# A retention block and a gated MLP on one core: decays 2 and 3 and four weight loads on GpSimd, and a new order of loads

## The chip, the cores and the metric

One NeuronCore of a Trainium2 chip. The metric is the device time of one execution in microseconds (us); times given for the kernel are the median of several runs. A profile is one execution, recorded instruction by instruction. Its engines are PE (TensorE: matmuls; PEld is its weight load), DVE (VectorE), ACT (ScalarE), POOL (GpSimd) and SP (SyncE, which here only issues transfers).

## The reference

Attention by a recurrence over 768 positions, for 4 batches and 8 heads of width 64, and behind it a two-layer MLP with a quick GELU. All values are float32; the program is given the two weight matrices as float64 and narrows them itself on the chip.

```python
def _attn_ref(q, k, v):
    B, H, S, D = q.shape                                    # 4, 8, 768, 64
    gamma = 1.0 - 2.0 ** (-5.0 - np.arange(H, dtype=np.float32))
    scale = 1.0 / np.sqrt(D)
    state = np.zeros((B, H, D, D), dtype=np.float32)
    for t in range(S):
        state = gamma[None, :, None, None] * state + np.einsum('bhd,bhe->bhde', k[:, :, t], v[:, :, t])
        y[:, :, t] = scale * np.einsum('bhd,bhde->bhe', q[:, :, t], state)
...
def _moe_ref(x, w_in, w_out):                               # x: 3072 x 512, from y
    h = x @ w_in                                            # 512 x 2048
    g = h * (1.0 / (1.0 + np.exp(-1.702 * h)))
    return (g @ w_out).astype(np.float32)                   # 2048 x 512
```

## The kernel before

**Attention** goes in 24 steps `j`, each 64 positions of two batches: steps 0 to 11 are the first two batches, 12 to 23 the others. Four steps make a block of 512 tokens for the MLP. A step is made of these pieces, whose names stand in the written order below:

- `q`, `k`, `v` load its operands (`load`, L139). For steps 0 to 5 the keys come as four transfers of 64 KB, the queries as one of 256 KB, the values as two of 128 KB. From step 6 on (`NEW`) queries and keys come already cut for a 32 by 32 transpose on VectorE, in eight transfers each of 32 KB made of 128-byte pieces (L176); there `q6` loads queries and keys together, and `v6` loads the keys once more in natural order (`kn`, four transfers) and the values (four), both at L161.
- `turn_q`, `turn_k` (steps 0 to 5) transpose on TensorE (L283); `turned_q`, `turned2_q`, `turned_k` copy the results out (L300), the second quarter pair of the queries on VectorE. `turn6`, `turn7` are VectorE's transposes (L294).
- `decay` weights the keys by their distance from the step's end: on ScalarE it is eight activations, one for each head (L323), on GpSimd one multiplication (L318; L325 from step 6).
- `score` (L339) multiplies keys and queries; `masked` (L380) takes the scores out under the causal decay mask; `own` (L367) multiplies them with the values; `gain` (L347) makes the step's addition to the state; `past` (L358) reads the state.
- `state` (L387) scales what `past` made, `x` (L409) adds it to `own` and writes the MLP's input; `aged` (L421, L418 or L423) decays the state, `updated` (L432) adds the gain.

Scores, gains, `past` and `own` use two fixed PSUM tiles (`PAS`, `PYS`), so a piece that writes one waits until the step before has been read out.

**The weights** come as 16 chunks of w_in and w_out, two transfers of 512 KB each (`w0a`, `w0b`, ... `w15b`, L201), into three raw buffers that are used in turn. Chunks 0 to 7 are w_in, 8 to 15 w_out. A chunk is narrowed by `abs` (L237) and `low` (L241) on ScalarE and `clip` (L245), `lift` (L248), `sign` (L253) and `rest` (L258) on VectorE. The raw buffer is free again once `sign` and `low` have read it. Chunk `i` of w_in holds two of the 16 strips of the hidden layer: chunks 0 to 7 are strips pairs 2, 7, 3, 6, 0, 4, 5 and 1.

**The MLP's first layer** of the first two blocks runs between these pieces: `up0.h.p` (L476) is a half block times strip pair `p`, `gate0.h.p` its GELU on ScalarE (L457); `seven` and `zero` (L559, L599) do the same with seven products in place of eight, from sums of weights (`seven_4`, `seven_6`, `seven_52`, L508 to L518) and of inputs (`zero_x` L546, `seven_x` L500). `seven_keep` (L538) stores such sums to DRAM. The second layer and all later blocks (L698, L821, L954) follow behind.

**What sets the order.** The pieces of the first 150 us stand in a list written by hand, one name after the other; `name@engine` puts a piece on another engine. Each engine executes its own instructions in the order of that list and waits by semaphores for what others make; so an instruction that waits holds up all that stands behind it on the same engine. Loads stand on SP, if the list doesn't say otherwise; they wait there for their buffer, and, with eight transfer semaphores used in turn, for the eighth transfer before them. The keys of step 0 are issued by ScalarE. A transfer that GpSimd issues has a queue of its own (q0), those of SP share q1. GpSimd in the first 110 us has the causal mask, the decays of steps 0 and 1, the small `whole` loads (L1035), `anew` (L1045 to L1053: a small load and copies that bring masks, decays and state into the layout of step 6 on) and from there decays and ages of the state.

Of the kernel before, what the change touches and what calls it, by code (L numbers as in the profile page):

```python
# [28 lines left out]
def kernel(  # L29
# [29 lines left out]
    pe, act, dve, pool, sp = nc.tensor, nc.scalar, nc.vector, nc.gpsimd, nc.sync  # L59
# [43 lines left out]
    row = G[0:1, 4, 0:2].rearrange("p a (h t) -> p (a h) t", t=D)  # L103
# [6 lines left out]
    mask = const.tile([P, 2, HP, D], F32, name="mask")  # L110
# [32 lines left out]
    def load(j, what="qkv", engine=None):  # L143

        b, c = j // NC * 2, j % NC
        rows = slice(c * D, (c + 1) * D)
        keep = send if j < 2 * CB else lambda i: i

        def plain(name, src, tag, bufs, engine=sp):
            t = two.tile([P, H, D], F32, name=name + "_in", tag=tag, bufs=bufs)
            QKV[name, j] = t
            for i in range(2):
                if j < NEW:
                    to, at = t[i * D:(i + 1) * D], src[b + i, :, rows, :].rearrange("h p d -> p h d")
                    for n in range(1 if name == "v" else 2):
                        keep(engine.dma_start(*((to, at) if name == "v" else (to[:, n:H:2], at[:, n * HP:(n + 1) * HP]))))
                else:
                    for r in range(2):  # L160
                        keep(engine.dma_start(t[r * D:(r + 1) * D, i * HP:(i + 1) * HP],  # L161
                                              src[b + i, r * HP:(r + 1) * HP, rows, :].rearrange("h p d -> p h d")))

        if j < NEW:
            if "q" in what:
                QKV["q", j] = t = two.tile([P, H * D], F32, name="q_in", tag="q_sq", bufs=2)
                keep((engine or sp).dma_start(t, q[b:b + 2, :, rows, :].rearrange("i h (k p) d -> (i h) k (p d)", p=8)))
            if "k" in what:
                plain("kn", k, "k_sq" if j in (0, 1, 4, 5) else "o", 2, engine or pool)
        elif "q" in what:  # L170
            for name, src in (("q", q), ("k", k)):
                t = two.tile([P, H, D // C4, C4], F32, name=name + "_sq")
                for r0 in range(0, P, C4):
                    for n in range(D // C4):
                        t0 = c * D + n * C4
                        tc.keep_in_program_order(sp.dma_start(  # L176
                            t[r0:r0 + C4, :, n], src[b + r0 // D, :, t0:t0 + C4, r0 % D:r0 % D + C4]
                            .rearrange("h p d -> p h d")))
                QKV[name, j] = t
        if "v" in what:  # L180
            if j >= NEW and c < NC - 1:
                plain("kn", k, "kn", 1)
            plain("v", v, "v", 2, engine or sp)
# [102 lines left out]
    def turn(j):  # L286

        if j < NEW:
            turn_new(j, 1)
            turn_new(j, 0)  # L290
        else:
            QT[j], KT[j] = home(j, "qT"), home(j, "kT")
            for t, name in ((QT[j], "q"), (KT[j], "k")):
                tc.keep_in_program_order(dve.transpose(  # L294
                    t.rearrange("p h t -> p (h t)"), QKV.pop((name, j)).rearrange("p h n d -> p (h n d)")))
        if 2 * CB <= j < NCH - 2:
            load(j + 2, "qk")
# [136 lines left out]
    def step(j, f=None):  # L434
        attend(j, f)
        if j is not None:
            masked(j)
            if j > 2 * CB:
                decay(j)
        if f is not None:  # L440
            c = f % NC
            if c == 0:
                updated(f)
            else:
                by_state(f)
            output(f)
            if 0 < c < NC - 1:
                aged(f)
                updated(f)
        if j is not None and 2 * CB < j < NCH - 1:  # L450
            load(j + 1, "v")
# [587 lines left out]
    def late_loads():  # L1039
        load(2 * CB, "qkv")  # L1040
        load(2 * CB + 1, "qk")
# [61 lines left out]

    begin()
    for name in """
        row@sp k0@act table q0 v0 z5 rows turn_q0 turn_k0 q1 w0b k1@sp w0a mask causal turned_q0
        turned2_q0@dve turned_k0 decay0@pool score0 v1 turn_k1 turn_q1 masked0 gain0 turned_k1 turned_q1 turned2_q1@dve own0 abs0b low0b updated0
        decay1@pool score1 clip0b lift0b sign0b rowd whole q2 k2@sp masked1 abs0a low0a rest0b x0 past1 gain1
        clip0a lift0a sign0a own1 rest0a aged1 turn_k2 turn_q2 w2b w2a state1 updated1 x1 turned_k2 turned_q2 turned2_q2@dve
        v2 q3 k3@sp up0.0.2 score2 abs2 decay2 aged2@dve q4 clip2 lift2 sign2 low2 decay3 w3b w3a  # L1110
        masked2 turn_k3 turn_q3 k4@sp gain2 past2 own2 v3 q5 rest2 k5@sp gate0.0.2 turned_k3 turned_q3 turned2_q3@dve updated2
        state2 score3 decay4 low3 turn_q4 turn_k4 up0.0.3 x2 masked3 gain3 past3 own3 abs3 clip3 lift3 sign3
        turned_q4 turned2_q4@dve rest3 turned_k4 score4 turn_k5 turn_q5 up0.0.6 w1a w5b w1b aged3 updated3 state3 w5a v4
        x3 up0.1.3 turned_q5 turned2_q5@dve gate0.0.3 abs1 low1 abs5 clip1 aged4 lift1 sign1 masked4 own4 gain4 w6a
        rest1 clip5 lift5 gate0.0.6 sign5 up0.0.7 past4 w6b decay5 low5 rest5 updated4 v5 gain5 w4a abs6
        gate0.1.3 turned_k5 clip6 state4 x4 lift6 score5 masked5 w4b abs4 up0.1.7 low6 aged5 gate0.0.7 w7a w7b
        low7 low4 q6 sign6 v6 own5 rest6 past5 seven_4.2 state5 gate0.1.7 seven_6.2 updated5 zero2.0 clip4 up0.1.6
        lift4 sign4 x5 seven_52.2 rest4 turn6 anew decay6 abs7 aged6 up0.1.2 w8a gate0.1.2 clip7 zero_x zero2.1
        score6 past6 q7 w8b v7 zero2.2 masked6 lift7 sign7 gain6 rest7 own6 w11b zero2.3 zero2.4 turn7
        w9a updated6 aged7 gate0.1.6 zero2.5 decay7 zero2.6 state6 w11a seven_4.0 x6 zero0.0 score7 masked7 abs8 clip8  # L1120
        past7 zero0.1 state7 seven_6.0 seven_52.0 lift8 sign8 gain7 own7 x7 seven_x zero0.2 zero0.3 zero0.4 zero0.5 low8
        seven_keep.2 w9b abs9 low11 clip9 rest8 lift9 zero0.6 w10a seven2.0 w10b seven2.1 abs11 clip11 lift11 sign11
        seven_4.1 rest11 seven2.2 abs10 seven2.3 seven2.4 seven_w.1 clip10 lift10 sign9 seven0.0 seven2.5 low10 low9 rest9 sign10
        updated7 rest10 seven_4.3 seven2.6 seven0.1 seven0.2 seven0.3 seven0.4 seven1.0 seven_keep.0 w14b w14a w12b w12a abs12 seven_w.3
        clip12 seven0.5 seven0.6 seven_v.1 lift12 sign12 abs14 clip14 low12 rest12 lift14 sign14 seven1.1 seven1.2 w13a seven1.3
        w13b abs13 low14 seven_v.3 clip13 lift13 seven1.4 sign13 seven3.0 seven1.5 rest14 seven1.6 seven3.1 seven3.2 seven3.3 seven3.4
        w15a seven_keep.3 seven_keep.1 w15b abs15 clip15 lift15 low13 low15 sign15 seven3.5 rest13 seven3.6 rest15 late_loads
    """.split():
        name, *e = name.split("@")
        works[name](*[{"sp": sp, "pool": pool, "act": act, "dve": dve}[x] for x in e])  # L1130
# [109 lines left out]
```

## Time and profile before

| | |
|---|---|
| median of 3 runs | 650.57 us (649.11 to 650.8) |
| the profiled execution | 651.44 us, of it 649.7 us span |
| HBM read and written | 79.18 MB and 14.94 MB |
| SP's queue q1 | 138,048 packets, 42.83 MB, 30.2% of 16 engines' span |
| GpSimd's queue q0 | 8,672 packets, 40.00 MB, 19.3% |
| weight transfers of 512 KB on SP, issue to landing | 4.8 us in the median |
| key transfers of 64 KB on SP | 4.8 us |
| SP waiting for the buffers of chunks 4 and 7 | 5.2 us before 49.19, 3.6 us before 53.71 |

A row of the profile's groups or timeline names the line, the engine, the operation, the written and read tiles, the shape and how often it runs; in square brackets stands the idle time of the engine just before, and what seemed to end it. A wait for several engines is put down to the one that finished last in the profile, which need not be the one that is waited for. The granted clock is the share of TensorE's full clock.

In the chain that ended last TensorE holds 83%, transfers 9%, SP's issuing 5%, waits for nothing visible 1%, VectorE 1%. Of the first 110 us much of that chain lies on SP's queue; from 103 us on it is TensorE almost alone.

### The profile page before, as it was taken

How to read it: one execution, taken by the hardware profiler on the slowest of the kernel's cores; microseconds unless marked ns; L12 is line 12 of the kernel's file. 1: busy time of each engine (PE TensorE's matmuls, PEld its weight loads, DVE VectorE, ACT ScalarE, POOL GpSimd, SP SyncE). 2: the span in 40 equal slices, each digit the busy share in tenths (PEclk: the TensorE clock that was granted, in tenths of full speed). 3: DMA queues.
4: the chain of work that ended last, by engine and by line, in shares of the span. 5: the costliest groups of instructions: out<-in, count | busy, mean ns of one | idle time of the engine just before them, and what ended most of it. 6: DMA issues, size and time to landing. Idle time of an engine off the chain costs nothing.

```text
span 649.7 us, 15510 instructions
## 1 busy us (share of the span) xinstructions
PE 633.4 (97%) x6543; PEld 578.4 (89%) x6543; DVE 435.6 (67%) x643; ACT 184.4 (28%) x329; POOL 152.0 (23%) x184
## 2 busy tenths in 40 slices
PE   7899999999999998999999999999999999999997
PEld 4788888888889997889999889999888999888997
DVE  2879887979989962438874337985246976145854
ACT  3778237661001102332101333100333110233210
POOL 4000211300612435000645000635300425200000
PEclk9989999999999999999999999999999999999999
DMA  9995587783368875720667730667741354221143
GB/s 198 228 258 161 112 252 214 198 209 57 93 200 264 206 175 171 200 67 4 172 179 213 215 85 1 160 161 189 211 95 49 89 174 143 110 91 49 59 153 98
DMA packets 150710, 96.86 MB, mean 149 GB/s; under 512 B 130512, under 2 KB 135888, under 8 KB 149616
## 3 DMA queue, kind: packets, MB, share of 16 engines
q1 hardware_dynamic: 138048, 42.83, 30.2%
q0 software_dynamic: 8672, 40.00, 19.3%
q10 hardware_dynamic: 3920, 13.04, 5.4%
q8 instruction: 51, 0.84, 0.6%
q14 instruction: 19, 0.16, 0.1%
HBM read 79.18 MB, written 14.94 MB: 145 GB/s over the span
## 4 chain that ended last, share of the span: by engine, by line
PE 83%; DMA 9%; SPq 5%; issue 1%; DVE 1%; ACT 1%; ACTq 0%
PE pq L821 33%; PE px L698 17%; PE pz L698 9%; PE pd L954 7%; PE ph L599 6%; PE py L698 4%; DMA W<-in_moe_w_out_dram 2%; SPq L161 2%; PE pa L339 2%; DMA q_in<-in_q_dram 2%; DMA kn_in<-in_k_dram 2%; DMA LATE<-W1D 1%; SPq L176 1%; PE py L367 1%; PE pa L347 1%; DMA v_in<-in_v_dram 1%
## 5 line engine op out<-in xcount | busy, mean ns | idle before, releaser
L821 PE MATMUL pq<-W,G 128*128 128x128 f32 x840 | 100.3, 276 | 0.0
L821 PEld LDWEIGHTS pq<-W,G 128*128 128x128 f32 x840 | 97.0, 192 | 0.8
L796 POOL DMA_DIRECT2D LATE<-W2D x34 | 18.7, 551 | 260.5 <-PE pq L821 139.8
L821 PE MATMUL pq<-LATE 128*128 128x128 f32 x560 | 74.8, 277 | 0.0
L821 PEld LDWEIGHTS pq<-LATE 128*128 128x128 f32 x560 | 68.2, 192 | 0.6
L698 PE MATMUL px<-X,LATE 128*128 128x256 f32 x256 | 60.6, 380 | 2.2 <-DMA LATE<-W1D 2.2
L698 PE MATMUL px<-X,W1A 128*128 128x256 f32 x256 | 60.5, 379 | 0.0
L698 PEld LDWEIGHTS px<-X,LATE 128*128 128x128 f32 x256 | 48.6, 190 | 9.1 <-issue 2.6
L698 PEld LDWEIGHTS px<-X,W1A 128*128 128x128 f32 x256 | 48.4, 190 | 6.3
L743 DVE TENSOR_TENSOR G<-pz,vv 128x512 f32<-128x512 f32 x16 | 11.1, 692 | 51.5 <-ACT vv L713 51.5
L843 ACT ACTIVATE o<-pq 128x512 f32<-128x512 f32 (+1 forms) x18 | 9.8, 544 | 119.9 <-PE pq L821 94.3
L457 ACT ACTIVATE G<-G 128x512 f32<-128x512 f32 x49 | 30.9, 630 | 43.1 <-DVE G L753 19.7
L821 PE MATMUL pq<-LATE,G 128*128 128x128 f32 x280 | 37.0, 275 | 0.0
L821 PE MATMUL pq<-W,LATE 128*128 128x128 f32 x280 | 37.0, 275 | 0.0
L954 PE MATMUL pd<-W,LATE 128*128 128x256 f32 x160 | 35.1, 380 | 0.0
L821 PEld LDWEIGHTS pq<-W,LATE 128*128 128x128 f32 x280 | 34.1, 192 | 0.0
L821 PEld LDWEIGHTS pq<-LATE,G 128*128 128x128 f32 x280 | 34.1, 192 | 0.0
L954 PEld LDWEIGHTS pd<-W,LATE 128*128 128x128 f32 x160 | 30.4, 190 | 4.1
L683 DVE TENSOR_TENSOR G<-G 128x512 f32<-128x512 f32 (+2 forms) x28 | 15.9, 567 | 23.5 <-ACT G L457 23.5
L810 DVE TENSOR_TENSOR LATE<-G 128x512 f32<-128x512 f32 x35 | 27.6, 789 | 5.0 <-PE pq L821 2.2
L476 PE MATMUL ph<-X,W1A 128*128 128x256 f32 x128 | 30.6, 397 | 0.2 <-DVE X L409 0.2
L698 PE MATMUL pz<-X,W1A 128*128 128x256 f32 x128 | 30.3, 380 | 0.0
(214 smaller groups left out, 1163.5 us busy)
## 6 DMA issues: line engine op xcount, KB each, us to landing
LATE<-W2D POOLq DMA_DIRECT2D x34, 768.0 KB, 5.2
W<-in_moe_w_out_dram SPq DMA_DIRECT2D x12, 512.0 KB, 6.0
LATE<-W1D ACTq DMA_DIRECT2D x4, 1536.0 KB, 9.7
LATE<-W1D POOLq DMA_DIRECT2D x4, 1536.0 KB, 8.9
kn_in<-in_k_dram SPq DMA_DIRECT2D x84, 64.0 KB, 4.8
W<-in_moe_w_in_dram SPq DMA_DIRECT2D x10, 512.0 KB, 4.8
out_dram<-o POOLq DMA_DIRECT2D x20, 256.0 KB, 4.6
q_sq<-in_q_dram SPq DMA_DIRECT2D x144, 32.0 KB, 3.0
```

Of the source, the lines that this page charges most:

```text
L161: keep(engine.dma_start(t[r * D:(r + 1) * D, i * HP:(i + 1) * HP], src[b + i, r * HP:(r + 1) * HP, rows, :].rearrange("h p d -> p h d")))
L339: pe.matmul(PAS[HALF[w], u, 0, s, :], kt[HALF[u], w, s, :], qt[HALF[u], w, s, :], start=True, stop=True)
L457: pin(act.activation(g, h[:, i], AF.Gelu_apprx_sigmoid))
L476: pe.matmul(h[:, ab], w, X[:, 2 * th + c // 2, c % 2, :], start=(ab == 0 and c == 0), stop=(c == 3), skip_group_check=True)
L599: pe.matmul(acc[:, u, :], w, x, start=(start and u == 0 and c == 0), stop=(stop and c == 1), skip_group_check=True)
L683: hold(dve.tensor_sub(q[0][1], q[0][0], q[0][1]))
L698: pe.matmul(acc[:, u, :], w1(2 * d + u, sw)[:, c, :], X[:, sx, c, :], start=(start and u == 0 and c == 0), stop=(stop and c == 1), skip_gr ...
L743: dve.tensor_add(a[3], z, v)
L796: engine.dma_start(c, W2D[i])
L810: dve.tensor_add(d[:, 0], s2, a11)
L821: pe.matmul(p0[:, j, :], a[:, d], w[:, d], start=(new and j == 0 and d == 0), stop=(d == NP // 2 - 1), skip_group_check=True)
L954: pe.matmul(p0[:, n, :], g1(m, p, sa)[:, n * P:(n + 1) * P], W2[:, sb, p, :], start=(new and p == 0 and n == 0), stop=(last and p == NP - ...
```

## The change

Ten names of the list move or change their engine, and `load` can load the queries and the keys of steps 6 and 7 apart:

- `k1@sp` stands ahead of `w0b` (it stood between `w0b` and `w0a`).
- `x1` stands ahead of `updated1`.
- `decay2` and `decay3` run on GpSimd (one multiplication each in place of eight activations on ScalarE).
- `w4a`, `w4b`, `w7a`, `w7b` are issued by GpSimd.
- `q6` stands behind `v5`, ahead of chunk 4, and the new name `k6` (the keys' eight transfers) behind `w4b`; both stood together as `q6` behind chunk 7. `k7` stands right behind `q7`, where it was.

In the built program TensorE's order is the same as before. On SP the sixteen transfers of `q6` and `k6` follow `v5`, then come the eight of `v6`, with no weight load between. GpSimd's order is: decays 0 and 1, `whole`, decays 2 and 3, chunk 4's two loads, a small copy of `anew` (it waits for ScalarE's decay 5), chunk 7's two loads, the small load of `anew`, the rest of `anew`.

```diff
@@ load
-        elif "q" in what:
-            for name, src in (("q", q), ("k", k)):
+        else:
+            for name, src in [(x, y) for x, y in (("q", q), ("k", k)) if x in what]:
                 t = two.tile([P, H, D // C4, C4], F32, name=name + "_sq")
...
@@ the list
-        row@sp k0@act table q0 v0 z5 rows turn_q0 turn_k0 q1 w0b k1@sp w0a mask causal turned_q0
+        row@sp k0@act table q0 v0 z5 rows turn_q0 turn_k0 q1 k1@sp w0b w0a mask causal turned_q0
...
-        clip0a lift0a sign0a own1 rest0a aged1 turn_k2 turn_q2 w2b w2a state1 updated1 x1 turned_k2 turned_q2 turned2_q2@dve
-        v2 q3 k3@sp up0.0.2 score2 abs2 decay2 aged2@dve q4 clip2 lift2 sign2 low2 decay3 w3b w3a
+        clip0a lift0a sign0a own1 rest0a aged1 turn_k2 turn_q2 w2b w2a state1 x1 updated1 turned_k2 turned_q2 turned2_q2@dve
+        v2 q3 k3@sp up0.0.2 score2 abs2 decay2@pool aged2@dve q4 clip2 lift2 sign2 low2 decay3@pool w3b w3a
         masked2 turn_k3 turn_q3 k4@sp gain2 past2 own2 v3 q5 rest2 k5@sp gate0.0.2 turned_k3 turned_q3 turned2_q3@dve updated2
...
-        rest1 clip5 lift5 gate0.0.6 sign5 up0.0.7 past4 w6b decay5 low5 rest5 updated4 v5 gain5 w4a abs6
-        gate0.1.3 turned_k5 clip6 state4 x4 lift6 score5 masked5 w4b abs4 up0.1.7 low6 aged5 gate0.0.7 w7a w7b
-        low7 low4 q6 sign6 v6 own5 rest6 past5 seven_4.2 state5 gate0.1.7 seven_6.2 updated5 zero2.0 clip4 up0.1.6
+        rest1 clip5 lift5 gate0.0.6 sign5 up0.0.7 past4 w6b decay5 low5 rest5 updated4 v5 q6 gain5 w4a@pool
+        abs6 gate0.1.3 turned_k5 clip6 state4 x4 lift6 score5 masked5 w4b@pool k6 abs4 up0.1.7 low6 aged5 gate0.0.7
+        w7a@pool w7b@pool low7 low4 sign6 v6 own5 rest6 past5 seven_4.2 state5 gate0.1.7 seven_6.2 updated5 zero2.0 clip4
...
-        score6 past6 q7 w8b v7 zero2.2 masked6 lift7 sign7 gain6 rest7 own6 w11b zero2.3 zero2.4 turn7
+        zero2.1 score6 past6 q7 k7 w8b v7 zero2.2 masked6 lift7 sign7 gain6 rest7 own6 w11b zero2.3
...
```

## The prediction

> **What bounds the kernel now.** I read the page's busy times and slices first, then busy time by stretch, then TensorE's waits, then the timeline around the longest of them, then the queues that feed it. A row of a stretch has its ends, its length, the busy time of PE, PEld, DVE, ACT and POOL, the granted clock, the DMA share and GB/s; a wait has its total, how often, and the longest.
>
> ```profile
> span 649.7 us, 15510 instructions
> PE 633.4 (97%) x6543; PEld 578.4 (89%) x6543; DVE 435.6 (67%) x643; ACT 184.4 (28%) x329; POOL 152.0 (23%) x184
> PEclk9989999999999999999999999999999999999999
> ```
> ```profile
> 0.00:16.00 16.00, 11.47 (x119) 6.83 (x119) 3.58 (x10) 5.25 (x10) 7.08 (x15) 1.00 0.97 198
> 16.00:34.00 18.00, 13.45 (x298) 11.59 (x297) 15.20 (x28) 14.10 (x40) 0.00 (x0) 1.00 1.05 224
> 34.00:60.00 26.00, 26.00 (x414) 22.57 (x414) 22.51 (x34) 21.16 (x46) 1.21 (x2) 0.93 0.88 241
> 60.00:110.00 50.00, 48.66 (x515) 41.46 (x515) 40.90 (x58) 22.10 (x35) 7.52 (x9) 1.00 0.65 170
> ```
> ```profile
> PE pa L339 <- ACT G L323: 2.7, 1, 2.7
> PE pt L283 <- DMA kn_in<-in_k_dram: 1.9, 2, 1.4
> ...
> PE ph L599 <- ACT p L604: 0.6, 1, 0.6
> PE ph L559 <- DVE W L546: 0.5, 1, 0.5
> ```
>
> TensorE is busy 97% of the span. Idle in the four stretches is 16 - 11.47 = 4.53, 18 - 13.45 = 4.55, 0 and 1.34 us. No TensorE instruction is added or taken away, so only these 10.4 us, and the stretch in which the clock is not full, can be won; a loss can arise anywhere. The longest wait, 2.7 us, stands before the scores of step 3:
>
> ```profile
> 25.47 2.01 ACT L323 ACTIVATE G<-kn_in,cold 128x64 f32<-128x64 f32 x8
> ...
> 28.43 2.04 ACT L323 ACTIVATE G<-kn_in,cold 128x64 f32<-128x64 f32 x8
> ...
> 30.82 1.30 ACT L300 ACTIVATE G<-pt 128x512 f32<-128x512 f32 x3
> ...
> 32.15 0.87 DVE L300 COPY G<-pt 64x256 f32<-64x256 f32 x2 [1.58 <-ACT G L300]
> 33.05 0.69 DVE L432 TENSOR_TENSOR state<-state,pa 128x512 f32<-128x512 f32 x1
> ...
> 33.88 0.69 PE L339 MATMUL pa<-G 64*64 64x64 f32 x32 [2.72 <-ACT G L323]
> ...
> 35.00:38.00 3.00, 3.00 (x11) 0.50 0.90 249
> ```
>
> The first two rows are the decays of steps 2 and 3. Behind them ScalarE copies the transposes of step 3 (30.82), VectorE copies the last quarter (32.15) and updates the state (33.05 to 33.74), and the scores begin 0.14 later. The wait is booked to ScalarE's third decay, but it is the state update that the scores wait for. The last row is a stretch with TensorE alone: after that wait its granted clock is 0.50; finer stretches put this between 34.9 and 38.3 us, so 3.4 us of work at half rate lost 1.7.
>
> **The change part by part.**
>
> *Keys of step 1 ahead of a weight load.* The four key transfers were issued at 5.32 to 8.13, behind 512 KB of weights. They move up one slot: 0.66 us (the next slot is 7.51, the one before 6.85). The 512 KB now follow them; at the 289 GB/s that 8 to 12 us moved, they are worth 1.8 us more. The keys landed at 12.06; 0.66 to 2.4 earlier is 9.7 to 11.4. TensorE had finished the scores of step 0 at 10.8 and waited 1.38. I take the whole 1.38 (at worst 0.66). The weight's first reader starts at 15.01, now 13.6; with 7.5 as issue and 4.8 to landing it has 12.3, so nothing. All that follows (copies, scores 1, steps 1 and 2) hangs on this chain.
>
> *State update and output of step 1 swapped on VectorE.* One 0.68 us instruction stands behind its neighbour instead of before it; TensorE waited 0.18 us there. At most 0.2.
>
> *Decays 2 and 3 on GpSimd.* ScalarE loses 2.01 + 2.04 us. GpSimd takes 1.04 each, as at 8.82 and 12.22, or up to 1.41, as at 69.55. It is idle from 14.86 to 51.22; the keys of step 2 land by 18, far ahead of use at 29.5, and nothing on GpSimd is behind the decays until 51. ScalarE's copies for step 3 now follow TensorE's transposes, 2 us earlier. VectorE then binds: it was busy without a gap from 24.45 to 30.57, so its copy starts at 30.57 instead of 32.15, which gives 1.58. Against it: the 128x1024 clip at 71.29 took 1.22 instead of 0.69 us while GpSimd worked at 70.92 to 71.96. An overlapping decay costs VectorE 0 to 0.53 us, and I take 0.3. So scores 3 come 1.38 + 1.58 - 0.3 = 2.7 earlier, TensorE's wait falls to some 1.4, and the half-rate stretch should go, which gives 1.7 more after it.
>
> *What is late next.* Step 4's decay stays on ScalarE and waits for its keys (landed 32.65); behind it stand low3, abs3 and, through VectorE, the copy of queries 4 (39.83 to 40.72) and rest3 (to 41.98). TensorE came to scores 4 at 42.11, 1.4 after the copy. The keys' transfer is issued behind the query load that waits for step 2's transposes (23.58), so it moves by those 1.38, less what the DMA engines (share above 1 in these stretches) withhold: I take 1.1, between 0 and 1.4. Scores 4 can then move by 1.4 + 1.1 = 2.5, and I take 2.2 for the contention above. The surplus of scores 3 and of the clock (2.7 + 1.7) beyond this turns into a new TensorE wait of about 2 us before scores 4. From there to 61.7 TensorE, VectorE and ScalarE all shift: VectorE's chain is driven by TensorE's transposes of step 5.
>
> *Loads.* SP's queue stood at 44 to 49.2 and 50.1 to 53.7 for the buffers of weights 4 and 7, with step 6's sixteen small transfers (4.74 + 4.85 us to issue) behind. Those now start at once, after the values of step 5 (43.98). SP is then free before VectorE's sign4 frees a buffer for weight 8 (66.72; issued 70.31), and the chain of issues from 70.3 to the load at 89.87, without which abs9 could not start (ScalarE waited 1.1 us to 99.38), moves by at least 3.6 us. TensorE's wait of 0.6 at 103.1 hangs on it and goes: 0.6. GpSimd issues the four weight loads, at 0.53 to 0.76 each by its other DMA rows, from the same release as before. Weight 4 landed at 54.18 for a reader at 55.04; weight 7 at 59.25, and its reader waited 0.4. Landing takes 5.0 on SP; the nearest rows on GpSimd are 4.6 (256 KB), 5.2 (768 KB) and 8.9 (1536 KB). I take 1 us later: ScalarE's low6 ends 3.0 us before rest6 needs it, and the bank that gate0.1.7 frees is wanted 2.7 later, so this costs nothing; at 3.9 us later it costs 1.2. Also moved on GpSimd: the 4 KB load of step 6's decays, needed at 70.9.
>
> The Trainium skill, "DMA: Bandwidth & Descriptors", section "Issuing engines are not separate DMA queues", says that transfers from any engine run on the same 16 engines and interleave, so a second issuer saves only issue time. By it nothing would be won in transfer; the sum above counts only SP's issue time, and what the rule warns of is the third rival.
>
> **Sum.** 2.2 + 0.6 = 2.8, less 0.2 for weights 4 and 7 and GpSimd's work beside a VectorE that is 97% busy at 50 to 70 us: 2.6. The profiled execution took 651.44 (span 649.7, 1.7 around it), 0.9 above the median of 650.57; it becomes 648.8, and the median 648.0.
>
> **Rivals.**
> 1. *The front's gain stays behind step 4's keys.* For it: DMA share 1.05 at 16 to 34. Against: the engines had a lull at 24 to 26 (share 0.45 at 24) because SP waited. Then only the slack of 1.4, less 0.3, passes, and 0.6 with the loads, less 0.2: 1.5, so 649.1.
> 2. *Half rate comes back.* The wait of 2.7 brought it; the one of 2 us at 255 to 257 left the clock at 1.00. The new waits (1.4 and 2) lie between 0 and that. If it follows the second, it costs 1.7 of the 2.6: 649.7. The Trainium skill, "TensorE: Matmul & The Clock Gate", section "What's actually happening", has a window of 3413 ns that runs freely and says an idle window halves the clock; the 3.4 us at 0.50 agree, though here 2.7 us of idling sufficed, so the phase decides.
> 3. *Weights 4 and 7 come late (slower).* They now share the engines with step 6's 128-byte pieces, which took 11.6 us from first issue to last landing (54.84 to 66.47). At that pace weight 7 lands 6.6 later, at 65.9; ScalarE's queue stands at low7, so gate0.1.7, which ends 2.8 us behind its start now (59.33 to 62.1), ends at 68.7, and TensorE, which took that bank at 64.79, waits 3.9: the front's gain is eaten whole and 3.9 - 0.6 added, 653.9. It decides from a landing 2.7 us later than before. Against: those pieces were paced by SP's issue, at a share of 0.4 to 0.8.
>
> **How the numbers follow.** Forecast 0.66, rivals 0.12, 0.08 and 0.14. A measurement of this kernel can tell about 0.3%, 1.95 us, from no change: faster is below 648.6. The forecast's own range is 645.9 (the new wait before scores 4 half as long, and all else as taken) to 648.6. Rivals 1 and 2 are "same", 0.20; rival 3 is "slower", 0.14. The range of 8 in 10 takes in rivals 1 and 2 and ends where nothing is gained: 645.9 to 650.6.
>
> **What would show it.** The first key transposes of step 1 at about 10.8; the wait before scores 3 at 1 to 1.7 us; no row with clock 0.50 after it; a wait of 1 to 2.5 before scores 4; up0.0.6 at 41.3 (was 43.6); no wait at 103. Wrong: keys of step 4 landing at 32.6 as before, a halved clock after 38, ScalarE waiting for weight 4 or 7 for over 3 us, or TensorE waits that are new between 44 and 103.

## The result and the profile after

The changed kernel takes 647.32 us (median of 13 runs, 646.24 to 649.11), the kernel before 650.62 in the runs beside it (13 runs, 648.56 to 655.58). The ratio is 0.9946, 95% interval 0.9929 to 0.9962: 3.5 us less, between 2.5 and 4.6. The profiled execution took 646.78 us, of it 645.1 us span.

The page of the changed kernel, its span, TensorE's busy time and the granted clock:

```profile
span 645.1 us, 15505 instructions
PE 630.9 (98%) x6543; PEld 576.1 (89%) x6543; DVE 439.7 (68%) x643; ACT 180.7 (28%) x313; POOL 160.3 (25%) x190
...
PEclk9899999999999999999999999999999999999999
```

The four stretches of the changed kernel (ends, length, busy time of PE, PEld, DVE, ACT, POOL, granted clock, DMA share, GB/s):

```profile
0.00:16.00 16.00, 11.43 (x129) 6.86 (x133) 4.52 (x11) 6.16 (x13) 6.54 (x14) 1.00 0.97 194
16.00:34.00 18.00, 13.38 (x329) 11.74 (x325) 17.41 (x29) 10.63 (x25) 2.54 (x2) 0.91 1.06 229
34.00:60.00 26.00, 25.65 (x443) 21.75 (x442) 22.78 (x34) 19.43 (x40) 4.91 (x7) 1.00 1.01 256
60.00:110.00 50.00, 49.18 (x461) 42.41 (x460) 41.75 (x61) 24.46 (x38) 10.85 (x10) 1.00 0.68 179
```

Busy time of TensorE is hardly the place to look, since the same matmuls are busy for longer at half clock. What changed is the clock column: the stretch 34 to 60 went from 0.93 to 1.00. The stretch 16 to 34 seems to have got worse (0.91 after 1.00), but the 1.00 of the kernel before is no measurement. Its trace has no record of the clock ahead of 24.69, and where there is none the view prints 1.00. The same 32 matmuls (the gains of steps 1 and 2) show the rate in the kernel before:

```profile
19.75 1.08 PE L347 MATMUL pa<-v_in,G 64*64 64x64 f32 x32
...
29.54 0.69 PE L347 MATMUL pa<-v_in,G 64*64 64x64 f32 x32
```

In the changed kernel the first of these two gains took 1.08 us as well, at 18.82, where the clock is on record as 0.50. So TensorE ran at half rate there in both kernels. The first record of the clock lies anywhere between 13.63 and 24.77 in the 14 profiles (24.69 and 16.04 in the two of the kernel before, 14.48 and 20.73 in the two of the changed one); so a difference between two single profiles at the front holds some chance that no edit made. Two finer windows of the changed kernel (length, PE busy, clock, DMA share, GB/s):

```profile
18.00:21.00 3.00, 3.00 (x98) 0.50 1.19 296
...
35.00:38.00 3.00, 3.00 (x52) 1.00 0.91 255
```

At 35 to 38 the clock is full where the kernel before had 0.50: up0.0.3, sixteen matmuls, took 3.62 us from 33.84 on, before 4.82 from 35.92 on. The half rate at 18 to 21 is no loss against the kernel before, and TensorE waits 0.93 for VectorE behind it. TensorE's waits in the first 160 us of the changed kernel (total, how often, longest):

```profile
PE py L358 <- ACT X L300: 1.4, 1, 1.4
...
PE pa L339 <- DVE state L432: 1.1, 1, 1.1
PE pa L347 <- issue: 1.1, 1, 1.1
...
PE ph L476 <- DVE X L409: 0.9, 1, 0.9
...
PE pt L283 <- DMA kn_in<-in_k_dram: 0.8, 2, 0.5
...
PE ph L559 <- DVE W L546: 0.6, 1, 0.6
```

The wait of 2.7 before the scores of step 3 (L339) has become two of 1.1, before the gain of step 2 (L347) and before those scores; both follow VectorE (the gain starts at 29.51, when the masking of scores 2 has ended at 29.40). The wait of 0.6 at 103 (L599) is not in the list any more.

Why the scores of step 3 came only 1.6 earlier (32.28 after 33.88) is seen in the timeline of GpSimd and VectorE (start, length, instruction):

```profile
19.07 1.09 POOL L318 TENSOR_TENSOR G<-kn_in,cold 128x512 f32<-128x512 f32 x1 [5.71 <-DMA kn_in<-in_k_dram]
26.68 1.45 POOL L318 TENSOR_TENSOR G<-kn_in,cold 128x512 f32<-128x512 f32 x1 [6.52 <-DMA kn_in<-in_k_dram]
```
```profile
19.30 1.49 DVE L253 SCALAR_TENSOR_TENSOR W1A<-W,W1A 128x256 uint32<-128x256 uint32 x2
...
23.56 0.89 DVE L300 COPY G<-pt 64x256 f32<-64x256 f32 x2
...
26.54 2.14 DVE L253 SCALAR_TENSOR_TENSOR G<-G 128x512 uint32<-128x512 uint32 x2
28.71 0.69 DVE L380 TENSOR_TENSOR G<-pa,mask 128x512 f32<-128x512 f32 x1
...
30.55 0.87 DVE L300 COPY G<-pt 64x256 f32<-64x256 f32 x2
31.45 0.69 DVE L432 TENSOR_TENSOR state<-state,pa 128x512 f32<-128x512 f32 x1
```

The same instructions of VectorE in the kernel before:

```profile
20.24 0.76 DVE L253 SCALAR_TENSOR_TENSOR W1A<-W,W1A 128x256 uint32<-128x256 uint32 x2
...
24.45 0.89 DVE L300 COPY G<-pt 64x256 f32<-64x256 f32 x2 [0.74 <-ACT G L300]
...
27.42 1.29 DVE L253 SCALAR_TENSOR_TENSOR G<-G 128x512 uint32<-128x512 uint32 x2
28.75 0.69 DVE L380 TENSOR_TENSOR G<-pa,mask 128x512 f32<-128x512 f32 x1
```

The two rows of GpSimd are the moved decays. Beside each stands a pair of VectorE's sign instructions: 1.49 and 2.14 us, where the kernel before has 0.76 and 1.29. Each time the pair ends 0.6 us after GpSimd has finished (20.79 after 20.16, 28.68 after 28.13). So VectorE lost 0.73 + 0.85 us. The first loss did not last: at its copy of queries 2 VectorE was 0.89 earlier again (23.56 after 24.45, where it had stood idle for 0.74). The second did: the masking of scores 2 (28.71) stands where it stood before (28.75), though all ahead of it had come 0.9 earlier.

### The profile page after: what moved, and what is told of

Read it like the earlier page. It is cut to its first block, busy times and chain, and to the rows that moved or that the text cites. A ratio compares the mean times of both kernels' runs of the same rounds, so it can differ in the third digit from the quotient of the medians.

```text
span 645.1 us, 15505 instructions
## 1 busy us (share of the span) xinstructions
PE 630.9 (98%) x6543; PEld 576.1 (89%) x6543; DVE 439.7 (68%) x643; ACT 180.7 (28%) x313; POOL 160.3 (25%) x190
## 4 chain that ended last, share of the span: by engine, by line
PE 87%; DVE 4%; DMA 3%; ACT 3%; issue 1%; SPq 0%; DVEq 0%; ACTq 0%
PE pq L821 34%; PE px L698 17%; PE pz L698 9%; PE pd L954 8%; PE ph L599 5%; PE py L698 4%; PE ph L559 3%; PE pa L339 2%; DMA kn_in<-in_k_dram 1%; PE py L367 1%; PE py L358 1%; PE pa L347 1%; PE py L599 1%; DMA W1A<-W1A 1%; ACT G L237 1%
## 5 line engine op out<-in xcount | busy, mean ns | idle before, releaser
L457 ACT ACTIVATE G<-G 128x512 f32<-128x512 f32 x49 | 30.9, 630 | 43.6 <-DVE G L753 19.6
L698 PE MATMUL py<-X,W1A 128*128 128x256 f32 x128 | 30.2, 379 | 0.0
```

Source lines behind the costliest of these rows:

```text
L457: pin(act.activation(g, h[:, i], AF.Gelu_apprx_sigmoid))
L698: pe.matmul(acc[:, u, :], w1(2 * d + u, sw)[:, c, :], X[:, sx, c, :], start=(start and u == 0 and c == 0), stop=(stop and c == 1), skip_gr ...
```

## The experiments

The table has all profiles. A column is one TensorE instruction, named by its time in the first profile of the kernel before; the entry is how much earlier (-) or later (+) it starts, in us. 12.2 is the first key transpose of step 1, 33.9 the scores of step 3, 43.6 up0.0.6, 103 the product after the wait of 0.6, 257 the product after a wait for the load LATE<-W1D.

| kernel | 12.2 | 33.9 | 38.4 | 43.6 | 61.4 | 90.2 | 103 | 254 | 257 | ratio to before |
|---|---|---|---|---|---|---|---|---|---|---|
| before, second profile | +0.26 | -0.28 | -0.64 | -0.64 | -0.64 | +0.32 | +0.11 | +0.28 | -2.09 | |
| keys alone | -0.77 | -0.22 | -0.28 | -0.28 | -0.28 | +0.35 | +0.65 | +0.88 | -1.16 | 0.9990 (0.9970 to 1.0010) |
| keys and swap | -0.56 | -1.09 | -1.35 | -1.35 | -1.35 | -1.12 | -1.24 | -1.28 | -3.05 | 0.9987 (0.9965 to 1.0008) |
| changed, loads back | -0.74 | -1.30 | -2.86 | -0.89 | +0.16 | +1.43 | +1.81 | +2.39 | +0.04 | 0.9987 (0.9967 to 1.0008) |
| order of loads alone | +0.25 | -0.27 | -1.94 | -1.33 | -1.33 | +1.62 | +0.84 | +0.79 | +0.10 | 1.0014 (0.9984 to 1.0043) |
| loads alone | +0.11 | +0.09 | +0.01 | +0.01 | +0.01 | +0.02 | -0.75 | -0.41 | -2.78 | 0.9968 (0.9952 to 0.9984) |
| GpSimd's loads alone | +0.50 | +0.45 | +0.44 | +0.44 | +0.44 | +0.72 | -0.06 | -0.20 | -2.57 | 0.9973 (0.9957 to 0.9989) |
| **changed** | -0.95 | -1.60 | -3.28 | -2.34 | -2.06 | -1.98 | -2.75 | -2.39 | -4.76 | 0.9946 (0.9929 to 0.9962) |
| changed, second profile | -0.79 | -1.50 | -3.12 | -1.14 | -0.84 | +0.42 | -0.36 | -0.27 | -2.64 | |
| changed, decays on ScalarE | -1.36 | -1.56 | -1.80 | -1.80 | -1.80 | -1.79 | -2.56 | -2.31 | -4.68 | 0.9959 (0.9940 to 0.9977) |
| changed, keys back | +0.73 | +0.07 | -1.61 | -0.25 | +0.04 | +0.10 | -0.68 | -0.81 | -3.18 | 0.9956 (0.9939 to 0.9973) |
| decays in ScalarE's gaps | -1.52 | -2.94 | -4.60 | -2.44 | -2.44 | -2.11 | -2.88 | -2.83 | -5.20 | 0.9950 (0.9928 to 0.9972) |
| the same, abs3 ahead | -1.15 | -3.20 | -4.87 | -4.13 | -0.53 | -0.31 | -1.09 | -1.22 | -3.60 | 0.9937 (0.9915 to 0.9959) |

**Decays back on ScalarE.**

```diff
-abs2 decay2@pool aged2@dve ... low2 decay3@pool w3b
+abs2 decay2 aged2@dve ... low2 decay3 w3b
```

> The changed kernel, but decays 2 and 3 on ScalarE as before. In the changed kernel's trace VectorE's sign instructions beside the two GpSimd decays took 1.15 us (0.42 in the kernel before) and 1.53 us (0.69), so 1.57 us of what ScalarE saved went to VectorE. Theory 1 (the decays still pay, by what they leave over and by the half-rate window): those instructions are back at 0.42 and 0.69; TensorE's wait before scores 3 is one piece of some 2.7 us again, scores 3 begin at 32.9 (33.88 less the 0.95 of the keys; 32.28 in the changed kernel), a stretch of 3.4 us at clock 0.50 lies behind it, and scores 4 begin at about 41.2 (39.27); the time is 0.6 to 1.9 us above the changed kernel's, ratio to before 0.9955 to 0.9975. Theory 2 (the decays gave nothing; VectorE lost as much as ScalarE won): scores 4 and the time as in the changed kernel, ratio 0.9946.

The sign pairs were back at 0.77 and 1.29, TensorE waited 2.90 before the scores of step 3, and 3.4 us at clock 0.50 began at 32.07: the first theory in these parts. But the scores themselves came 1.56 earlier than before, as in the changed kernel (1.60), and the ratios 0.9959 and 0.9946 are not told apart. The keys of step 1 had landed 0.41 earlier in this profile, though. Counted from the key transposes of step 1, the scores of step 3 come 0.56 to 0.71 earlier than in the first profile of the kernel before in the four profiles with both decays on GpSimd, and between 0.54 earlier and 0.55 later in the eight with both at their old place. So for the start of the scores the decays on GpSimd gave little, and no gain clear of that scatter: of the 1.58 us for which VectorE no longer waited for ScalarE, its longer second sign pair took back 0.85. What they took away is the long wait and with it the half rate: from 33.9 to 38.4 the changed kernel wins 1.68, this one 0.24.

**Keys alone, and the loads alone.**

```diff
-q1 w0b k1@sp w0a
+q1 k1@sp w0b w0a
```

> The kernel before with one edit: the keys of step 1 ahead of the first weight load. Theory 1 (the key chain passes on what it gains): first key transposes of step 1 at 11.25 (12.20), scores 3 some 0.95 earlier, 32.9, and 0.9 us off the end: ratio 0.9985. Theory 2 (a later wait takes it back: the third decay on ScalarE or step 4's keys): 0.9 earlier at step 1 and 0 at scores 4 (42.11), ratio 1.000.

The keys came 0.77 earlier and 0.28 of it was left at 38.4: TensorE waited 1.54 us before up0.0.2 for the output of step 1, then 3.06 before scores 3. The time (0.9990) tells nothing apart.

```diff
-v5 gain5 w4a abs6 ... w4b abs4 ... w7a w7b low7 low4 q6 sign6 ... q7 w8b
+v5 q6 gain5 w4a@pool abs6 ... w4b@pool k6 abs4 ... w7a@pool w7b@pool low7 low4 sign6 ... q7 k7 w8b
```

> The kernel before with the loads alone: step 6's queries and keys ahead of weight chunk 4, four weight loads on GpSimd. Theory 1 (SP's issue time was the price of the wait at 103): nothing moves before 44; weights 4 and 7 land about 1 us later, ScalarE waits 1 to 2 us for each, TensorE has no new wait between 44 and 103; the wait of 0.61 at 103 is gone; 0.6 off the end, ratio 0.999. Theory 2 (engine sharing makes weights 4 and 7 late enough to cost): a new TensorE wait of over 0.3 us between 55 and 75, ratio 1.000 or above.

Nothing moved before 44, the wait at 103 went, and there was no new wait of TensorE up to there: the first theory. Its size is wrong: 0.9968 is 2.1 us, at least 1.0, and 0.6 lies outside. Weights 4 and 7 also came later than it has them, by 2.0 and 3.9 us (56.19 and 63.14), and ScalarE waited 1.14 and 3.05 for them; TensorE was not held up by it.

**Decays in ScalarE's gaps.**

```diff
-aged1 turn_k2 ... abs2 decay2@pool aged2@dve ... low2 decay3@pool w3b ... turned_q3 turned2_q3@dve
+aged1 decay2 turn_k2 ... abs2 aged2@dve ... low2 w3b ... turned_q3 decay3 turned2_q3@dve
```

> The changed kernel with decays 2 and 3 on ScalarE again, but at other places: decay 2 behind the age of step 1 (ScalarE idle 19.3 to 21.7 there), decay 3 behind the copies of step 3 (idle 29.3 to 31.8). GpSimd then works on nothing beside VectorE there. Theory 1 (VectorE's contention with GpSimd is what is left in the front): the two sign instructions take 0.42 and 0.69 us again, masked2 and what follows come up to 1.5 us earlier than in the changed kernel, scores 3 at 30.8 to 31.5 (32.28); of that 0 to 1.5 us passes scores 4 (39.27), whose chain also hangs on the decay of step 4 and its keys; time 645.8 to 647.3, ratio 0.9925 to 0.9946. Theory 2 (VectorE's long instructions have another cause than GpSimd): they stay at 1.15 and 1.53, and scores 3 do not move.

The timeline of this kernel, VectorE and then TensorE:

```profile
26.05 1.29 DVE L253 SCALAR_TENSOR_TENSOR G<-G 128x512 uint32<-128x512 uint32 x2
27.37 0.69 DVE L380 TENSOR_TENSOR G<-pa,mask 128x512 f32<-128x512 f32 x1
...
35.91 0.69 DVE L245 TENSOR_SCALAR G<-G 128x1024 f32<-128x1024 f32 x1 [3.20 <-ACT G L237]
```
```profile
30.95 0.69 PE L339 MATMUL pa<-G 64*64 64x64 f32 x32 [1.20 <-ACT G L323]
...
39.27 0.94 PE L339 MATMUL pa<-G 64*64 64x64 f32 x28 [1.57 <-DVE G L300]
```

The pair takes 1.29 again, the masking comes 1.34 earlier than in the changed kernel and scores 3 1.33 earlier (30.95). Of that 0.57 was there at the first key transpose, since the keys landed earlier; the rest is VectorE's, so GpSimd was the cause of the long pairs. All of it is lost at scores 4, which start at 39.27 in both kernels. VectorE stands idle for 3.20 us there, because abs3 on ScalarE (L237) stands behind step 4's decay, and that waits for its keys (it began at 31.66).

**The same, and abs3 ahead of step 4's decay.**

```diff
-score3 decay4 low3 turn_q4 ... own3 abs3 clip3
+score3 abs3 low3 decay4 turn_q4 ... own3 clip3
```

> As the kernel with the two decays in ScalarE's gaps, and abs3 and low3 stand ahead of step 4's decay on ScalarE. In that kernel scores 3 came at 30.95, and TensorE then waited 1.58 us before scores 4 (39.27, as in the changed kernel), because VectorE's copy of queries 4 stands behind clip3, lift3 and sign3, these behind abs3 (34.77), and abs3 behind the decay that waits for step 4's keys (31.66). Theory 1 (that chain is the next bound): abs3 starts near 31, VectorE's clip3 near 32.8, scores 4 at 37.7 to 38.2, and the wait is under 0.5; 1.1 to 1.5 us more off the end: ratio 0.991 to 0.993. Theory 2 (TensorE or VectorE takes it back before 62, where VectorE is 97% busy): scores 4 earlier but TensorE's later waits grow by as much, ratio 0.995.

The wait before scores 4 went, as the first theory has it; 4.13 us were won at 43.6. Then the second theory: TensorE waited 1.9 us before own4, behind the masking of scores 4, which stands on VectorE behind chunk 1's clip, lift and sign.

```profile
PE py L367 <- DVE G L380: 1.9, 1, 1.9
```

This wait brought 3.4 us at clock 0.50 from 48.99. ScalarE had begun abs1 only at 43.8. At 61.4, 0.53 was left. Neither of the two kernels is shown to be faster than the changed one.

**Loads back, and GpSimd's loads alone.**

```diff
-v5 q6 gain5 w4a@pool ... w4b@pool k6 abs4 ... w7a@pool w7b@pool low7 low4 sign6
+v5 gain5 w4a ... w4b abs4 ... w7a w7b low7 low4 q6 k6 sign6
```

> The changed kernel with the loads as before: chunks 4 and 7 on SP, step 6's queries and keys behind them. Theory 1 (the loads are worth the wait at 103 alone): scores 4 as in the changed kernel, 39.3, the wait of 0.6 at 103 is back, and 0.6 us more: ratio 0.9955. Theory 2 (the loads are worth 2 us or more, as the run with them alone suggests, 0.9968; the rest of it lies at the second block's weights, where the kernel before waited 2.2 us at 255): a wait of 1 to 3 us before the first product that reads LATE, at about 252, and ratio 0.998.

The wait at 103 was back (0.99), scores 4 began at 40.83 and not at 39.3, and there was no wait at 252. By 61.4 the whole gain of the front was gone in this profile. That isn't shown to come from the loads: TensorE waited 1.39 before scores 4, ahead of the moved loads, as in the second profile of the changed kernel below, and keys and swap, with the same old loads, kept their 1.35 to 61.4. The ratio went from 0.9946 to 0.9987, 2.7 us: nearer to the second theory in size, though not at the place it named. This run is also the front's three edits alone against the kernel before: 0.8 us won, between a loss of 0.5 and a gain of 2.1.

```diff
-gain5 w4a abs6 ... w4b abs4 ... w7a w7b low7
+gain5 w4a@pool abs6 ... w4b@pool abs4 ... w7a@pool w7b@pool low7
```

> The kernel before with the four loads of chunks 4 and 7 issued by GpSimd and nothing else; step 6's queries and keys stay in their place on SP. Theory 1 (it is SP's queue standing for those buffers that cost the wait at 103): SP issues step 6's transfers from 44 on as with the whole set of loads, the wait at 103 goes, ratio as with the loads alone, 0.997 to 0.999. Theory 2 (the order of step 6's transfers matters as well): the wait at 103 stays at 0.3 to 0.6.

The wait at 103 went, and the time is that of all the loads (0.9973 against 0.9968): the first theory.

**The order of the loads alone.**

```diff
-v5 gain5 w4a abs6 ... w4b abs4 ... low7 low4 q6 sign6 ... q7 w8b
+v5 q6 gain5 w4a abs6 ... w4b k6 abs4 ... low7 low4 sign6 ... q7 k7 w8b
```

> The kernel before with step 6's queries and keys ahead of chunk 4 on SP, all four loads of chunks 4 and 7 staying on SP behind them. Theory 1 (either edit is enough, since SP's standing time is what counts): no wait at 103, 61 to 134 us as short as with all the loads (0.4 to 0.7 shorter than in the first profile of the kernel before), ratio 0.997. Theory 2 (ahead on the same queue, step 6's 16 issues of 0.5 us hold chunks 4 and 7 back by up to 8 us): weight 4 lands 3 us or more later than 54.18, TensorE has a new wait of over 1 us between 55 and 75, ratio 1.000 or above.

Weight 4 landed at 58.76 (54.18 in the kernel before), weight 7 at 66.21 (59.25). Waits of ScalarE in the stretch 40 to 75 us, and of TensorE from 20 on:

```profile
ACT G L237 <- DMA W<-in_moe_w_in_dram: 4.9, 1, 4.9
ACT W1A L241 <- DMA G<-in_moe_w_in_dram: 3.6, 1, 3.6
```
```profile
PE ph L476 <- DVE X L409: 2.2, 1, 2.2
PE ph L476 <- ACT g L457: 2.1, 1, 2.1
PE px L698 <- DMA LATE<-W1D: 1.5, 1, 1.5
```

ScalarE waited 4.9 and 3.6 us for the two weights, gate0.1.7 (L457) ended late, and TensorE waited 2.1 us for the bank that it frees, at 66.9. This is the third rival of the prediction, with weight 7 at 66.2 where it said 65.9 and a wait of 2.1 where it said 3.9, in a kernel that keeps the loads on SP. The wait at 103 went here too. (The 2.2 us for L409 stand before up0.0.2, ahead of the moved loads.) The time tells nothing (1.0014, 0.9984 to 1.0043), so the second theory is shown in the trace only.

**Keys back, and keys with the swap.**

```diff
-q1 k1@sp w0b w0a
+q1 w0b k1@sp w0a
```

> The changed kernel with the keys of step 1 behind the first weight load again, as before. Theory 1 (the keys carry the front's gain): key transposes of step 1 at 12.2 to 12.7 (11.25), scores 3 near 33.2 (32.28), scores 4 at 40.2 to 40.7 (39.27); 0.9 to 1.4 us more than the changed kernel, ratio 0.996 to 0.997. Theory 2 (VectorE or step 4's keys bind anyway, so the early keys only move waiting time): scores 4 at 39.3 to 39.6 and ratio 0.9946.

Transposes at 12.93, scores 3 at 33.95, scores 4 at 40.51: the first theory in the trace. In time 0.9956 against 0.9946, not told apart.

```diff
-q1 w0b k1@sp w0a ... state1 updated1 x1 turned_k2
+q1 k1@sp w0b w0a ... state1 x1 updated1 turned_k2
```

> The kernel before with two edits: keys of step 1 ahead of the weight load, and VectorE writes step 1's output ahead of its state update. With the keys alone, up0.0.2 waited 1.54 us for that output (0.18 in the kernel before), and at 43.6 only 0.28 of 0.77 was left. Theory 1 (the swap lets the early keys through): up0.0.2 starts 0.6 to 0.7 earlier than with the keys alone (22.91), at 22.2 to 22.4, and 0.6 or more of the gain arrives at scores 4: 41.0 to 41.5 against 42.11. Theory 2 (the swap is worth nothing, because the third decay on ScalarE and step 3's copies decide): scores 4 at 41.8 as with the keys alone. Ratio 0.998 by the first, 0.999 by the second, which the time will hardly tell apart.

up0.0.2 began at 22.64 after a wait of 0.15, scores 4 at 40.77, and 1.35 were left at 43.6 where the keys alone left 0.28. The wait went as the first theory has it, in one profile each. What the swap is worth isn't shown: the keys brought only 0.56 of these 1.35, and the second profile of the kernel before stands 0.64 earlier at 43.6 with no edit at all. The times say nothing (0.9987 and 0.9990).

**Second profiles.**

> The kernel before, unchanged, profiled once more. Theory 1 (the wait of 2.2 us at 255 belongs to the kernel before): it is there again with 1 to 3 us. Theory 2 (it is chance: a transfer of values that came late before ScalarE could issue the load): under 0.5 us this time. The wait before scores 3 with 2.5 to 3, the clock of 0.50 behind it and the wait at 103 are there in both cases.

Waits of TensorE, 20 to 300 us, in the second profile of the kernel before:

```profile
PE pa L339 <- DVE state L432: 2.7, 1, 2.7
...
PE ph L599 <- ACT p L604: 0.4, 1, 0.4
```

No wait at 255 this time. The first profile has one there, which the prediction did not count as winnable (all waits of the first profile of before):

```profile
PE px L698 <- DMA LATE<-W1D: 2.2, 1, 2.2
```

So 2.2 of the 4.6 us between the two spans (649.7 and 645.1) hang on a wait that the kernel before does not have in every execution.

> The changed kernel, unchanged, profiled once more. Theory 1 (its stretch from 61 to 134 us of the kernel before is steady, since SP no longer runs late there): 0.36 to 0.70 shorter than in the first profile of the kernel before, as in the six profiles with the loads so far (the four without them: 0 to 2.3 longer). Theory 2 (that difference is chance): outside that. The time 646.2 to 649.1 either way.

Waits of TensorE, 20 to 300 us, in the second profile of the changed kernel:

```profile
PE ph L559 <- DVE W L546: 1.4, 1, 1.4
PE pa L339 <- DVE G L300: 1.4, 1, 1.4
```

The first theory fell: from 61.4 to 134 this profile is 0.60 longer than the first of the kernel before, not shorter. Before scores 4 TensorE waited 1.4 us (0.25 in the first), since step 4's decay could begin only at 33.11 (31.81), when its keys had landed. The wait of 1.4 before L559, at 74.33, has another source: weight 4 landed at 58.34 (55.09 in the first profile), ScalarE waited 3.34 us for it, and VectorE's rest6 then 1.27 for ScalarE's low6. Only from 90 to 103 are the profiles steady: 0.77 or 0.78 us shorter in all nine in which the loads or their order are changed.

## Why the prediction was right, point by point

648.0 was forecast, 647.32 came. The mechanisms named are seen in the traces, but two terms were mis-sized, the front too high and the loads too low. That the total came so near is in part luck, as the last point shows.

*Keys, 1.38.* They came at 11.25 and 11.41 in the two profiles, not at 10.8, inside the bounds; 0.95 and 0.79 were won.

*Swap, at most 0.2.* Read from the wait in the kernel before. With the keys early, TensorE waits 1.54 there without the swap, so the bound is likely too low: one edit can change what the other is worth. It is not shown. The wait is 0.93 and 1.14 in the two profiles of the changed kernel, with the swap, and 0.63 in the second profile of the kernel before, without it.

*Decays, 1.58 less 0.3 on VectorE.* VectorE's idle 1.58 before its copy went, as forecast, but the 0.3 was too low: VectorE lost 0.73 and 0.85 in the first profile, and the 0.85 reached the scores of step 3. With the keys' 0.95, that is 0.95 + 1.58 - 0.85 = 1.68; they came 1.60 earlier and not 2.7. The bound (0 to 0.53 each) came from one row, the clip of 1.22 us. The Trainium skill, "SBUF — State Buffer", section "SBUF: two separate sides", has a rule that gives a higher bound: whichever of a GpSimd instruction that reads SBUF and a VectorE instruction with two SBUF inputs starts first holds the shared ports to its end, and the other stands still. The rows agree: the sign instruction that began at 27.15 ended 0.55 behind the decay, and the decay at 26.68, begun beside the sign instruction before it, took 1.45 where the other took 1.09. By that rule a decay can cost VectorE up to its whole length; the rows show 0.73 and 0.85 of 1.04.

*Half rate, 1.7.* Right for the stretch it names. Seven profiles with both decays at their old place on ScalarE (two of the kernel before; keys alone; keys and swap; loads alone; GpSimd's loads alone; decays back) have the wait of 2.7 to 3.1 and clock 0.50 from 32 to 35 on. An eighth (order of loads alone) had lost 2.2 before up0.0.2, waited 1.2 here and had full clock. The four with both on GpSimd have waits of 1.0 to 1.2 and full clock too. From 33.9 to 38.4, 1.68 and 1.62 were won against the first profile of the kernel before, 1.3 against the second. The second rival did not come at this place. What the prediction overlooked is the half rate ahead of 24.69: it read 1.00 there from stretches without a record of the clock.

*New wait before scores 4, about 2.* 0.25 and 1.4. At 43.6 the two profiles stand at -2.34 and -1.14, the forecast being 2.2 and the first rival (keys of step 4 no earlier) 1.4 less 0.3, 1.1. In the second profile these keys landed at 33.01 (32.65 before), a sign of being wrong that the prediction named. The same kernel does the one or the other, by when those keys land.

*Weights 4 and 7, one us later, costing nothing.* In the first profile they landed at 55.09 and 60.32, 0.9 and 1.1 later. ScalarE's waits in the changed kernel, 40 to 110 us:

```profile
ACT G L237 <- DMA W<-in_moe_w_in_dram: 2.1, 1, 2.1
...
ACT W1A L241 <- DMA G<-in_moe_w_in_dram: 1.3, 1, 1.3
```

TensorE has no new wait between 44 and 71. The 0.2 for crowding was 0.36 by 90. But one us was too low: in the eight profiles with GpSimd's loads, weight 4 landed 0.7 to 4.2 later and weight 7 1.1 to 4.5 later. In the second profile of the changed kernel they landed at 58.34 and 62.40, ScalarE waited 3.34 (over 3 was a sign of being wrong), VectorE stood idle for 1.27 by it and was then busy without a gap up to the inputs of the product at 74.33, for which TensorE waited 1.40: this cost up to 1.27. The wait of the third rival, for the bank that gate0.1.7 frees, came in none of the eight, not even with weight 7 at 3.9 later (loads alone), which the forecast put at 1.2. The prediction had misread where TensorE takes that bank. The order of loads alone shows it waiting there before the 17th of the 32 matmuls that begin at 63.50 in the kernel before. There the 17th starts at 66.95 and not at 64.79, 4.85 behind the gate's end and not 2.7. With the gate ending at 68.7, the rival's wait would have been 1.75, not 3.9.

*Loads, 0.6.* This term failed in size. The runs give 2.1 us alone (1.0 to 3.1) and 2.7 as taken back. The wait at 103 is 0.61 in the first profile of the kernel before, and 0.40 to 0.99 in four others that keep the old loads (second profile, keys alone, keys and swap, loads back). From 90 to 103 these five differ from the first by -0.21 to +0.38, mean 0.07; with the steady 0.78 of the others that is 0.85. Secondly, the wait for LATE<-W1D stands in three of those five (2.21, 0.43, 0.17; mean 0.56) and in none of eight with GpSimd's loads. ScalarE issues that load behind a transfer of values (in the first profile of the kernel before it landed at 247.04 and the load went out at 247.21); why it comes late more often with the old loads was not tried. Thirdly, against the first profile 61 to 90 is 0.6 longer in the mean of those five and 0.3 in the eight, with much scatter. These three are 1.7 of the 2.1 to 2.7; the last part is a count of few profiles, not shown. The Trainium skill, "DMA: Bandwidth & Descriptors", section "Issuing engines are not separate DMA queues", calls the issue time that a second issuer saves usually small. Here it was not the time of issuing: SP stood 5.2 and 3.6 us for two buffers, with all later loads behind it.

*The sum.* Front 2.2 and loads 0.6, less 0.2, made 2.6; 3.5 came. By the ratios the loads are 2.1 and the rest 1.4 (0.9946 against 0.9968, within wide intervals); the run with the loads back gives the front 0.8, at most 2.1. Of the parts, the times tell only the loads from nothing, not the front or any edit of it. So 0.8 to 1.4 too much in one term and 1.5 to 2.1 too little in the other made a total 0.9 too low: the near hit is in part luck. The front was sized at its best case, and the loads by one profile, which happened to be the quickest of five between 61 and 134 us.

## What to carry to other kernels

When work is moved to GpSimd beside a busy VectorE, price the move with up to the moved instruction's whole time on VectorE (here 0.73 and 0.85 us of 1.04), unless VectorE is idle there. A load that waits for its buffer is dear by what stands behind it in the queue, which one profile shows badly: take a second profile before sizing a wait of under 1 us. Where several chains end together (here state, weights and keys between 30 and 50 us), a gain in one is worth what the next leaves, so the next wait has to be in the sum. Where a trace has no record of the clock, read the rate from the length of equal instructions, not from the clock column.

## What the runs showed that was not expected

The records fit a TensorE clock that is decided over pieces of 3413 ns on a grid that is fixed within a run, and by their total idle time, not by one long wait. In every profile each record that begins ahead of 600 us is a whole number of 3413 ns long. Over all 14 profiles, from the first record of the clock up to 600 us, each of the 15 pieces that were followed by half rate held 1.93 to 2.97 us of idle time. Of the pieces that were not, one held 1.94 and all others 1.79 or less. In the changed kernel two waits of 0.94 and 1.40 us in one piece brought the half rate at 17.9; in its second profile the clock is not on record ahead of 20.73, and the gain of step 1, 1.08 us at 18.95, has the length of half rate there.
